# Half of w_out prepared in the first FFN layer, and the second layer's operands kept in trace order: an attention, MoE and FFN chain on one Trainium2 core

## The chip, the cores and the metric

One NeuronCore of one Trainium2 chip runs one launch of the kernel. The metric is the device time of that core in microseconds (us); lower is better. The engines are TensorE (PE; its weight loads are PEld), VectorE (DVE), ScalarE (ACT), GpSimd (POOL) and SyncE (SP), which here only issues DMAs. ScalarE issues DMAs too.

## The reference

Three stages follow one another, all in float32.

```python
def _attn_ref(q, k, v, omega):              # 4 batches, 8 heads, 576 tokens, 64 wide, 128 features
    q_p, k_p = phi(q * scale), phi(k * scale)   # phi: exp(proj - |x|^2/2 - max) / sqrt(m)
    kv = np.einsum('bhsm,bhsd->bhmd', k_p, v)
    num = np.einsum('bhsm,bhmd->bhsd', q_p, kv)
    den = np.einsum('bhsm,bhm->bhs', q_p, z)[..., None] + 1e-06
    return num / den

def _moe_ref(x, w_gate, w1, w2):            # x 2304 x 512, 8 experts, 512 -> 1024 -> 512, top 1
    for e in range(E):
        xe = x[expert_idx == e]
        out[mask] = gate_w[mask, None] * (np.maximum(xe @ w1[e], 0.0) @ w2[e])

def _moe2_ref(x, w_in, w_out):              # 2304 x 512, w_in 512 x 2048, w_out 2048 x 512
    h = x @ w_in
    g = h * (1.0 / (1.0 + np.exp(-1.702 * h)))
    return g @ w_out
```

The weights w_in and w_out of the last stage lie in HBM as 8-byte floating point numbers.

## The kernel before

**Stages.** The attention and the MoE of earlier batches are interleaved on TensorE until some 346 us from the span's start (a batch's MoE takes the one expert that most of its tokens chose, for all its tokens; tokens of other experts would go through a loop at the end, which does not run with these inputs). The MoE of the last batch ends at 420 us. Then the last stage runs as two layers: the first layer (x by w_in, then the gate function) until 601 us, the second (by w_out) until 794 us.

**The two layers.** Both use a two by two block scheme with 7 products in place of 8, and each product takes three fp32r matmuls (high by high, high by low, low by high part), so that every operand is split into a high part, made by a ScalarE copy (L817), and a low part, made by a VectorE subtraction (L818), by the helper `split`. The first layer has 8 column groups j and 3 token sets t: 24 pairs of 42 matmuls with 384 columns, written by `first(j, t)` (L1097). The second has 9 token blocks k of 168 matmuls with 256 columns, 24 for each product, written by `second(k)` (L1198). For block k the operands are the parts of g (tiles gt and pg, read back from g_dram): a11, a12, a22 as they are, and sums and differences of them (`made`, L1184). The order of products in both layers is 1, 7, 5 (or 6), 6, 2, 4, 3; `ops[n]` are the two halves of product n's operand, in the tiles gs and p.

**Preparing the weights.** An 8-byte number is turned into a float32 by three integer operations on VectorE (L789, L794 and L798, in `decoding`). `prep_ins` does this for w_in, column group by column group, mixes the blocks (L864, `tt`) and splits them into wi. `prep_outs` does it for w_out: for each of 8 groups j, two loads (raw_o), 2 times 3 decoding operations of 128x512, four mixes (L864, z from z) of 128x256, and two stores from z to wo_dram (L926, L927). z and raw_o live in the pool wz, whose two tiles later hold the wi of group 0. `prep_w(i)` (L1153) later loads one product's w_out operand from wo_dram (p or pw) and splits it; it waits, when the kernel is written out, until all 8 groups are done (`outs[0] < NP`).

**What sets the order.** A list of generators (`Runner`, `jobs`) is advanced one tick at a time from the loops that write out the matmuls; in the first layer there are 7 ticks per pair. Each `yield n` in a generator lets n ticks go by. Behind this a scheduler reorders the instructions of each engine by its own estimate, except those that `behind(ins, n)` keeps behind the last n instructions that were written before them on their engine (HOLD is 1). In `second` the operands are held in this way for blocks 0 to 2 only (`HOLD if k < 3 else 0`), and the VectorE half of `split` never is. All loads of w_out and the stores to wo_dram are on SP's queue; the stores of g (g_dram) are on ScalarE's queue. `g` tiles of the first layer (tag "ob") rotate through three buffers, and a buffer is free again when the store of the g that it held has landed. y_t[t] are the operands of token set t; the loop over `order` waits (in writing) for wi of j and y of t.

**Matmuls.** In the first layer a pair of the products' writes goes `pa`, `pq`, `pf` and so on (PSUM tiles qa, qm, qn or qt, qu); VectorE adds two of them into g or qn or qt (L864), ScalarE applies the gate function (L1105).

In `second(k)` the four leading steps (`ops[1]`; s1; a21; `ops[7]`) of block k+1 are written in step 6 of block k, its last product:

```python
                if step == 6 and k + 1 < NB2:
                    for _ in range(4):
                        next(blocks[k + 1])
```

## Time and profile before

| | |
|---|---|
| Time, median of 3 runs (us) | 798.47 (793.82 to 801.49) |
| The profiled execution (us) | 802.5 |
| Its span in the trace (us) | 800.7 |
| TensorE busy | 755.4 us, 94% of the span |
| VectorE busy | 530.4 us, 66% |
| ScalarE busy | 340.4 us, 43% |
| GpSimd busy | 132.5 us, 17% |

The profiled execution is one more run than the three, and its time has 1.8 us outside the span. Times in rows are microseconds from the span's start. A busy engine is one with an instruction in progress; the idle time in square brackets behind a row is that just before it on its engine, with what ended it. PEclk is the clock that TensorE was granted, as a share of 2.4 GHz; it has two levels, 0.5 and 1. L numbers are lines of the kernel before; in the changed kernel the same lines are one further from about line 818 on, and more later.

### The profile page before, as it was taken

Reading aid. Unit: us, or ns where it says so; the run is one execution under the profiler, and the core shown is the slowest. Engines: PE = TensorE matmul, PEld = TensorE weight load, DVE = VectorE, ACT = ScalarE, POOL = GpSimd, SP = SyncE. Lnnn points to the kernel's source line nnn. Section 1 sums busy time; section 2 is a strip of 40 time slices with the busy share of each in tenths; the row PEclk is TensorE's granted clock in tenths of the full one; section 3 lists DMA queues with packets and bytes.
Section 4 is the critical chain, followed back from the end, with each engine's and each line's share of the span. In section 5 each row is a group of like instructions: output and inputs, shape, how many; then the busy total and the mean of one; then the engine's idle time right before and its main releaser. Section 6 shows DMA issues by size and latency. Waiting matters only on the chain.

```text
span 800.7 us, 14405 instructions
## 1 busy us (share of the span) xinstructions
PE 755.4 (94%) x5589; PEld 728.7 (91%) x5589; DVE 530.4 (66%) x1178; ACT 340.4 (43%) x643; POOL 132.5 (17%) x78
## 2 busy tenths in 40 slices
PE   7998899996999898999999999999999989999996
PEld 6877799996999888999999999998999889999996
DVE  5867786576988775435869825544358677777761
ACT  5545562343423422243417644544566233433330
POOL 4554295356300422000000000000000000000000
PEclk9989899999899999999999999999999989999999
DMA  6446674268864864167236435443779343444211
GB/s 157 128 111 170 197 216 121 74 165 241 243 183 157 215 237 137 50 185 240 74 123 202 161 119 173 149 178 119 289 276 318 116 132 120 144 130 135 80 27 31
DMA packets 135724, 126.59 MB, mean 158 GB/s; under 512 B 57568, under 2 KB 120288, under 8 KB 134752
## 3 DMA queue, kind: packets, MB, share of 16 engines
q1 hardware_dynamic: 128736, 106.72, 44.6%
q10 hardware_dynamic: 6912, 18.88, 6.2%
q8 instruction: 46, 0.75, 0.4%
q14 instruction: 30, 0.25, 0.1%
HBM read 78.69 MB, written 40.39 MB: 149 GB/s over the span
## 4 chain that ended last, share of the span: by engine, by line
PE 45%; DVE 5%; DMA 3%; issue 1%; ACT 1%; DVEq 0%; ACTq 0%; SPq 0%
PE qa L1198 12%; PE qa L1097 11%; PE qm L1198 7%; PE m_ps L126 3%; PE pb L1198 3%; PE qm L1097 3%; PE qu L1097 2%; PE w_ps L126 2%; DMA g_dram<-g 2%; PE qn L1097 1%; PE qt L1097 1%; DVE y L818 1%; DVE p L818 1%; DMA gt<-g_dram 1%; DVE gs L818 1%
## 5 line engine op out<-in xcount | busy, mean ns | idle before, releaser
L1097 PE MATMUL qa<-y,wi 128*128 128x384 f32 x576 | 109.0, 336 | 3.5 <-DVE g L864 2.1
L1097 PEld LDWEIGHTS qa<-y,wi 128*128 128x128 f32 x576 | 100.2, 188 | 5.7 <-DVE g L864 3.4
L126 PE MATMUL m_ps<-xh,wh 128*128 128x288 f32 x256 | 80.4, 314 | 1.8 <-DVE h1l L698 1.7
L126 PE MATMUL m_ps<-xh,wl 128*128 128x288 f32 x256 | 78.1, 305 | 0.0
L126 PE MATMUL m_ps<-xl,wh 128*128 128x288 f32 x256 | 77.7, 304 | 0.0
L663 POOL TENSOR_TENSOR wl<-st,wh 128x1024 fp32r<-128x1024 f32 x23 | 55.5, 2421 | 111.3 <-ACT wh L661 111.2
L347 DVE TENSOR_REDUCE small<-pr 128x4 f32<-128x512 f32 (+1 forms) x80 | 51.1, 639 | 10.3 <-PE pr L339 3.9
L126 PEld LDWEIGHTS m_ps<-xh,wh 128*128 128x128 f32 x256 | 50.3, 196 | 3.0 <-DVE h1l L698 2.9
L661 ACT ACTIVATE wh<-st 128x1024 fp32r<-128x1024 f32 (+1 forms) x33 | 34.0, 1033 | 39.6 <-DMA st<-in_moe_w_dram 33.0
L126 PEld LDWEIGHTS m_ps<-xl,wh 128*128 128x128 f32 x256 | 50.2, 196 | 0.1
L126 PEld LDWEIGHTS m_ps<-xh,wl 128*128 128x128 f32 x256 | 49.9, 195 | 0.2
L695 ACT ACTIVATE h1h<-m_ps 128x288 fp32r<-128x288 f32 x64 | 25.8, 406 | 56.3 <-PE m_ps L126 56.2
L698 DVE SCALAR_TENSOR_TENSOR h1l<-m_ps,h1h 128x288 fp32r<-128x288 f32 x64 | 28.7, 452 | 30.1 <-ACT h1h L695 29.9
L126 PE MATMUL m_ps<-h1h,wh 128*128 128x288 f32 x160 | 48.4, 303 | 0.0
L126 PE MATMUL m_ps<-h1l,wh 128*128 128x288 f32 x160 | 47.9, 300 | 0.0
L126 PE MATMUL m_ps<-h1h,wl 128*128 128x288 f32 x160 | 47.7, 299 | 0.0
L1198 PE MATMUL qa<-p,p 128*128 128x256 f32 x360 | 45.8, 284 | 1.1 <-DVE p L818 0.9
L1198 PEld LDWEIGHTS qa<-p,p 128*128 128x128 f32 x360 | 44.3, 192 | 1.6 <-DVE p L818 1.1
L1198 PE MATMUL qa<-p,gs 128*128 128x256 f32 x360 | 45.3, 283 | 0.0
L1198 PEld LDWEIGHTS qa<-p,gs 128*128 128x128 f32 x360 | 44.1, 192 | 0.0
L432 PEld LDWEIGHTS num<-kv,qpT 128*128 128x128 f32 (+1 forms) x320 | 37.5, 187 | 6.3 <-ACT qpT L420 2.7
L432 PE MATMUL num<-kv,qpT 128*128 128x65 f32 (+1 forms) x320 | 40.1, 269 | 3.0 <-ACT qpT L420 1.0
(208 smaller groups left out, 1845.8 us busy)
## 6 DMA issues: line engine op xcount, KB each, us to landing
g_dram<-g ACTq DMA_DIRECT2D x48, 384.0 KB, 2.6
st<-in_moe_w_dram SPq DMA_DIRECT2D x31, 512.0 KB, 5.4
pg<-g_dram SPq DMA_DIRECT2D x10, 1024.0 KB, 5.7
raw_o<-in_moe_w_out_dram SPq DMA_DIRECT2D x16, 512.0 KB, 3.9
raw<-in_moe_w_in_dram SPq DMA_DIRECT2D x16, 512.0 KB, 4.4
gt<-g_dram SPq DMA_DIRECT2D x8, 1024.0 KB, 5.5
wo_dram<-z SPq DMA_DIRECT2D x8, 768.0 KB, 6.5
p<-wo_dram SPq DMA_DIRECT2D x6, 1024.0 KB, 7.5
```

The costliest lines, as they stand in the source:

```text
L126: ins = nc.tensor.matmul(out=ps, lhsT=a, rhs=b, start=start and n == 0, stop=stop and n == 2)
L347: nc.vector.tensor_reduce(out=pm, in_=ps[:, :w], axis=AX.X, op=ALU.max, negate=on_act)
L432: nc.tensor.matmul(out=ps[:n, c, h2, :], lhsT=lhsT, rhs=kv[:, h, :])
L661: nc.scalar.activation(out=hi[:, :, s], in_=st[:, :, s], func=ACTF.Copy)
L663: eng.tensor_tensor(out=lo[:, :, s], in0=st[:, :, s], in1=f32(hi)[:, :, s], op=ALU.subtract)
L695: nc.scalar.activation(out=hh[:, f], in_=ps, func=ACTF.Relu)
L698: nc.vector.scalar_tensor_tensor(out=hl[:, f], in0=ps, scalar=0.0, in1=f32(hh[:, f]), op0=ALU.max, op1=ALU.subtract)
L818: nc.vector.tensor_tensor(out=lo, in0=src, in1=f32(hi), op=ALU.subtract)
L1097: ins = nc.tensor.matmul(out=ps, lhsT=w[:, a, ks], rhs=y[:, b, kk], start=start and kk + m == 0, stop=kk == 1 and m == 2, skip_group_check ...
L1198: ins = nc.tensor.matmul(out=ps, lhsT=x[:, f], rhs=w[i][:, f], start=start and f + m == 0, stop=f == NP - 1 and m == 2, skip_group_check=True,
```

## The change

It has five parts.

1. `prep_outs` takes its groups, its tiles and its queue as arguments. Groups 0 to 3 are prepared in the attention, from tick 245 of its clock on instead of from the first finished batch on, with loads and stores on ScalarE's queue. Groups 4 to 7 are prepared in the first layer, on SP's queue, in the tile that held yt, from the moment y_t[2] is made. Each group has three stores instead of two.
2. `prep_ins` starts its loads and its decoding without waiting for w_out; it waits for groups 0 to 3 before it writes to wi. Its pace goes from 8 to 6 ticks, and it yields after every second mix.
3. The first nine pairs are done set by set, (0,0), (1,0), (2,0), (0,1) and so on, instead of (0,0), (1,0), (0,1), (1,1), (2,0).
4. In `second` both halves of an operand, and the sums, are held in trace order for all blocks. The four leading steps of a block are written two in step 5 and two in step 6 of the block ahead.
5. The paces of `prep_w` for the third and fourth operand go from 10 and 13 to 7 and 9.

```diff
+    NP1 = 4
+    OUT_FROM = 245
-    IN_PACE = 8
+    IN_PACE = 6
...
-    def split(hi, lo, src, n=0):
+    def split(hi, lo, src, n=0, n_lo=0):
         behind(nc.scalar.activation(out=hi, in_=src, func=ACTF.Copy), n)
-        nc.vector.tensor_tensor(out=lo, in0=src, in1=f32(hi), op=ALU.subtract)
+        behind(nc.vector.tensor_tensor(out=lo, in0=src, in1=f32(hi), op=ALU.subtract), n_lo)
...
-        while outs[0] < NP:
-            yield 1
         raw = [load(0, 0), load(1, 0)]
...
-            while j % 3 >= len(slots["wi"]) or (j > 2 and through[j - 3] < NSET):
+            while j % 3 >= len(slots["wi"]) or (j > 2 and through[j - 3] < NSET) or outs[0] < NP1:
                 yield 1
...
+    def prep_outs(js, qs, ts, raws, queue, gap):
...
+            behind(queue.dma_start(out=raws[n], in_=w_out[f * P:(f + 1) * P, :]), 1)
...
+            for o, n, x in ((0, 1, q[:, 0:1]), (1, 2, q[:, 2:4]), (3, 4, ts)):
+                behind(queue.dma_start(out=wo_dram[o:o + n, :, j].rearrange("o p d -> p o d"), in_=x), 1)
             outs[0] += 1
-            yield OUT_PACE
+            yield gap
...
-            if x_done[0]:
+            if clock[0] >= OUT_FROM:
                 jobs()
...
             def made(out, x, y, op):
-                behind(nc.vector.tensor_tensor(out=out, in0=x, in1=y, op=op), HOLD if k < 3 else 0)
+                behind(nc.vector.tensor_tensor(out=out, in0=x, in1=y, op=op), HOLD)
...
-                split(gs[:, 0], gs[:, 1], x, n)
+                split(gs[:, 0], gs[:, 1], x, HOLD, HOLD)
...
-        order = [(0, 0), (1, 0), (0, 1), (1, 1), (2, 0), (2, 1), (0, 2), (1, 2), (2, 2)]
+        order = [(j, t) for t in range(NSET) for j in range(3)]
...
         def after_group(j, t):
+            if "late" not in slots and 2 in y_t:
+                slots["late"] = p = ly.tile([P, ZW], F32, tag="yt", name="pz", bufs=1)
...
+                jobs.queue.append(prep_outs(
+                    range(NP1, NP), (z[:, 0:4], z[:, 4:8]), z[:, 8:12], (raws[:, 0], raws[:, 1]), nc.sync, 3
+                ))
...
-                jobs.queue += [prep_w(2, p[:, 0:WO], 10), prep_w(3, p[:, WO:2 * WO], 13)]
+                jobs.queue += [prep_w(2, p[:, 0:WO], 7), prep_w(3, p[:, WO:2 * WO], 9)]
...
-                if step == 6 and k + 1 < NB2:
-                    for _ in range(4):
+                if step > 4 and k + 1 < NB2:
+                    for _ in range(2):
                         next(blocks[k + 1])
+                if step == 6:
                     if k + 2 < NB2:
                         gts[k + 2] = load_g(k + 2)
```

Three places show what moves.

On VectorE in the attention, the rows of the kernel before where the first group of w_out begins (mx, qp, small: steps of the attention's features; z: w_out):

```order
L347 TENSOR_REDUCE small<-pr 128x4
L789 TENSOR_SCALAR z<-raw_o 128x512
L356 TENSOR_TENSOR small<-small,sq 128x4
L794 SCALAR_TENSOR_TENSOR z<-raw_o,z 128x512
L356 TENSOR_TENSOR mx<-small,sq 128x4
L798 SCALAR_TENSOR_TENSOR z<-raw_o,z 128x512
L368 TENSOR_TENSOR qp<-pr,mx 128x512
```

and the same place in the changed kernel:

```order
L348 TENSOR_REDUCE small<-pr 128x4
L357 TENSOR_TENSOR small<-small,sq 128x4
L357 TENSOR_TENSOR mx<-small,sq 128x4
L369 TENSOR_TENSOR qp<-pr,mx 128x512
L348 TENSOR_REDUCE small<-pr 128x2
```

The three z rows between the feature steps are gone from here; the changed kernel's first z row stands about 150 VectorE rows further on, between rows of the MoE (h1l).

On ScalarE in the MoE of the last batch, the rows of the changed kernel that read the staged expert weights (wh) and its hidden part (h1h); the kernel before has the wh and h1h rows alone:

```order
L908 DMA raw_o_233<-in_moe2_w_out_dram 128x512 x2
L662 ACTIVATE wh0_4380<-st_4158 128x1024
L696 ACTIVATE h1h_4343<-m_ps_4404 128x288
L696 ACTIVATE h1h_4343<-m_ps_4423 128x288
L662 ACTIVATE wh1_4419<-st_4179 128x1024
L696 ACTIVATE h1h_4343<-m_ps_4440 128x288
L926 DMA wo_dram_77<-z_232 128x256
L662 ACTIVATE wh2_4455<-st_4402 128x1024
L696 ACTIVATE h1h_4343<-m_ps_4459 128x288
L926 DMA wo_dram_77<-z_232 128x2x256
L662 ACTIVATE wh3_4491<-st_4438 128x1024
```

Loads of w_out and stores to wo_dram now stand in ScalarE's own order, each store ahead of a split that TensorE needs.

On VectorE in the second layer, the rows of the kernel before around the seventh operand of block 2 (p0 from pg is its low half; s1_7276 is a sum of block 2, s1_7481 and the gt1 rows are the leading steps of block 3):

```order
L1184 TENSOR_TENSOR s1_7276<-pg_6524 128x1024
L1211 TENSOR_TENSOR ob_7216<-qm_7136,pg_6524 128x256
L1184 TENSOR_TENSOR s1_7481<-gt1_6892 128x1024
L1184 TENSOR_TENSOR pg_6524<-pg_6524 128x8x128
L1211 TENSOR_TENSOR ob_7215<-qa_7163,pg_6524 128x256
L818 TENSOR_TENSOR p1_6714<-s1_7276,p1_6714 128x1024
L1184 TENSOR_TENSOR gt1_6892<-gt1_6892 128x8x128
L818 TENSOR_TENSOR gs_6851<-pg_6524,gs_6851 128x1024
L818 TENSOR_TENSOR p0_6523<-pg_6524,p0_6523 128x1024
```

and in the changed kernel (the names' numbers are 9 higher):

```order
L1185 TENSOR_TENSOR s1_7259<-pg_6533 128x1024
L1212 TENSOR_TENSOR ob_7225<-qm_7145,pg_6533 128x256
L1185 TENSOR_TENSOR pg_6533<-pg_6533 128x8x128
L1212 TENSOR_TENSOR ob_7224<-qa_7172,pg_6533 128x256
L819 TENSOR_TENSOR p0_6532<-pg_6533,p0_6532 128x1024
L819 TENSOR_TENSOR p1_6723<-s1_7259,p1_6723 128x1024
L1185 TENSOR_TENSOR s1_7259<-s1_7259,pg_6533 128x1024
```

Between the difference a21 (pg from pg) and the low half of the seventh operand (p0 from pg) stood four other rows, one of them block 3's (gt1) and one the low half of a later operand (p1); now one stands there.

## Rows read from the trace of the kernel before

**Rows 1.** The head of the page and its engines (busy us, share, instructions).

```profile
span 800.7 us, 14405 instructions
...
PE 755.4 (94%) x5589; PEld 728.7 (91%) x5589; DVE 530.4 (66%) x1178; ACT 340.4 (43%) x643; POOL 132.5 (17%) x78
```

**Rows 2.** Stretch, length, busy (instructions) of PE, PEld, DVE, ACT, POOL; PEclk, DMA share, GB/s.

```profile
187.00:262.00 75.00, 68.83 (x589) 65.79 (x589) 67.27 (x201) 25.78 (x54) 17.98 (x8) 0.95 0.67 203
262.00:346.00 84.00, 77.27 (x582) 73.87 (x581) 52.57 (x153) 25.33 (x52) 19.76 (x8) 0.96 0.52 157
420.20:601.10 180.90, 177.35 (x1014) 175.02 (x1013) 98.98 (x162) 99.24 (x187) 0.00 (x0) 1.00 0.52 184
601.10:794.40 193.30, 186.85 (x1513) 185.43 (x1511) 135.93 (x146) 74.75 (x86) 0.00 (x0) 0.97 0.40 127
```

**Rows 3.** What TensorE waited for (total us, times, longest).

```profile
PE tq L418 <- DVE qp L368: 9.9, 6, 4.6
...
PE qm L1198 <- DVE p L818: 3.3, 1, 3.3
...
PE qm L1198 <- DVE gs L818: 1.8, 1, 1.8
```

**Rows 4.** Timeline of TensorE, 193.5 to 200.5 us.

```profile
199.13 1.09 PE L418 MATMUL tq<-ident,qp 128*128 128x128 f32 x4 [4.62 <-DVE qp L368]
```

**Rows 5.** Timeline of VectorE, 192 to 200 us.

```profile
191.72 2.12 DVE L789 TENSOR_SCALAR z<-raw_o 128x512 int32<-128x512 int32 x1 [0.31 <-DMA raw_o<-in_moe_w_out_dram]
...
193.87 2.72 DVE L794 SCALAR_TENSOR_TENSOR z<-raw_o,z 128x512 int32<-128x512 int32 x1
...
198.30 0.68 DVE L368 TENSOR_TENSOR qp<-pr,mx 128x512 f32<-128x512 f32 x1
```

**Rows 6.** The tile z: one operation's durations (min, median, max ns).

```profile
L794 DVE SCALAR_TENSOR_TENSOR z<-raw_o,z x16: 672/683/2718, 193.9 to 322.9; 128x512 int32<-128x512 int32 x16
```

**Rows 7.** Timeline of GpSimd, 192 to 200 us.

```profile
193.50 2.54 POOL L663 TENSOR_TENSOR wl<-st,wh 128x1024 fp32r<-128x1024 f32 x1
```

**Rows 8.** Stretches behind waits, columns as in rows 2.

```profile
199.13:205.10 5.97, 5.97 (x33) 5.81 (x33) 5.90 (x17) 2.30 (x4) 2.38 (x1) 0.50 0.71 210
...
628.40:631.90 3.50, 3.46 (x16) 3.46 (x17) 2.38 (x3) 1.06 (x1) 0.00 (x0) 0.52 0.02 4
...
653.86:659.00 5.14, 5.14 (x24) 5.14 (x25) 3.43 (x3) 1.06 (x1) 0.00 (x0) 0.50 0.51 164
659.00:679.00 20.00, 20.00 (x168) 20.00 (x168) 13.13 (x15) 7.85 (x9) 0.00 (x0) 1.00 0.41 129
270.00:273.40 3.40, 3.40 (x17) 3.40 (x16) 3.40 (x7) 1.47 (x2) 2.26 (x1) 0.50 0.55 142
```

**Rows 9.** Timeline of TensorE at three waits of the two layers.

```profile
430.28 2.02 PE L1097 MATMUL qa<-y,wi 128*128 128x384 f32 x10 [0.92 <-DVE g L864]
...
544.07 0.61 PE L1097 MATMUL qa<-y,wi 128*128 128x384 f32 x2 [1.10 <-ACT wi L817]
...
653.86 1.44 PE L1198 MATMUL qm<-p 128*128 128x256 f32 x5 [3.27 <-DVE p L818]
```

**Rows 10.** Timeline of VectorE, 645.5 to 654.5 us.

```profile
651.45 1.22 DVE L818 TENSOR_TENSOR gs<-pg,gs 128x1024 fp32r<-128x1024 f32 x1
652.59 1.22 DVE L818 TENSOR_TENSOR p<-pg,p 128x1024 fp32r<-128x1024 f32 x1
```

**Rows 11.** Timeline of VectorE at the first layer's end, 583 to 602 us.

```profile
599.32 0.55 DVE L864 TENSOR_TENSOR g<-qa,qs 128x384 f32<-128x384 f32 x1
```

**Rows 12.** Timeline of VectorE, 264 to 276 us.

```profile
266.62 0.43 DVE L789 TENSOR_SCALAR z<-raw_o 128x512 int32<-128x512 int32 x1 [3.78 <-DMA wo_dram<-z]
```

**Rows 13.** Timeline of VectorE, 480 to 505 us.

```profile
487.41 0.56 DVE L864 TENSOR_TENSOR g<-qa,qs 128x384 f32<-128x384 f32 x1 [3.05 <-DMA g_dram<-g]
```

**Rows 14.** Timeline of GpSimd, 262 to 313 us.

```profile
262.05 4.71 POOL L663 TENSOR_TENSOR wl<-st,wh 128x1024 fp32r<-128x1024 f32 x2 [48.11 <-ACT wh L661]
```

**Rows 15.** Timeline of ScalarE, 340 to 372 us.

```profile
354.91 1.06 ACT L661 ACTIVATE wh<-st 128x1024 fp32r<-128x1024 f32 x1 [4.25 <-DMA st<-in_moe_w_dram]
```

More of the change, by code (lines that the diff above doesn't have):

```diff
@@ L885, in prep_ins @@
             s1, s2, s4 = (mix[:, i] for i in range(3))
-            for o, x, y, op in (
+            for n, (o, x, y, op) in enumerate((
                 (s1, dec[:, WS3], dec[:, W22], ALU.add), (dec[:, WS3], dec[:, W11], dec[:, WS3], ALU.subtract),
                 (s2, s1, dec[:, W11], ALU.subtract), (s4, dec[:, W12], s2, ALU.subtract),
-            ):
+            )):
                 behind(tt(nc.vector, o, x, y, op), HOLD)
-                yield 1
-            while j % 3 >= len(slots["wi"]) or (j > 2 and through[j - 3] < NSET):
+                if n % 2:
+                    yield 1
+            while j % 3 >= len(slots["wi"]) or (j > 2 and through[j - 3] < NSET) or outs[0] < NP1:
                 yield 1
@@ L902 @@
     outs = [0]
-    def prep_outs():
-        z = wz.tile([P, 8 * HD], F32, tag="a", name="z", bufs=1).rearrange("p (o d) -> p o d", o=8)
-        zi = z.bitcast(I32)
-        raws = wz.tile([P, 2, DM], I64, tag="b", name="raw_o", bufs=1)
+    def prep_outs(js, qs, ts, raws, queue, gap):
         def load(n, j):
             f = j + n * NP
-            behind(nc.sync.dma_start(out=raws[:, n], in_=w_out[f * P:(f + 1) * P, :]), 2)
-        load(0, 0)
-        load(1, 0)
+            behind(queue.dma_start(out=raws[n], in_=w_out[f * P:(f + 1) * P, :]), 1)
+        load(0, js[0])
+        load(1, js[0])
         yield 8
-        for j in range(NP):
+        for i, j in enumerate(js):
+            q = qs[i % len(qs)]
+            qi = q.bitcast(I32)
             for n in range(2):
-                yield from decoding(zi[:, 2 * n:2 * n + 2].rearrange("p a c -> p (a c)"), raws[:, n])
-            for i, (o, a, b, op) in enumerate(O_MIX):
-                if j + 1 < NP and not i % 2:
-                    load(i // 2, j + 1)
-                behind(tt(nc.vector, z[:, o], z[:, a], z[:, b], op), HOLD)
+                yield from decoding(qi[:, 2 * n:2 * n + 2].rearrange("p a c -> p (a c)"), raws[n])
+            z = [q[:, o] for o in range(4)] + [ts[:, o] for o in range(4)]
+            for m, (o, a, b, op) in enumerate(O_MIX):
+                if m % 2 and i + 1 < len(js):
+                    load(m // 2, js[i + 1])
+                behind(tt(nc.vector, z[o], z[a], z[b], op), HOLD)
                 yield 1
             yield 1
-            behind(nc.sync.dma_start(out=wo_dram[0, :, j], in_=z[:, 0]), 2)
-            behind(nc.sync.dma_start(out=wo_dram[1:7, :, j].rearrange("o p d -> p o d"), in_=z[:, 2:8]), 1)
+            for o, n, x in ((0, 1, q[:, 0:1]), (1, 2, q[:, 2:4]), (3, 4, ts)):
+                behind(queue.dma_start(out=wo_dram[o:o + n, :, j].rearrange("o p d -> p o d"), in_=x), 1)
             outs[0] += 1
-            yield OUT_PACE
+            yield gap
     def prep_y(t, home, after=0):
@@ L976 @@
         jobs = Runner(4)
-        jobs.queue.append(prep_outs())
+        z = wz.tile([P, 8 * HD], F32, tag="a", name="z", bufs=1).rearrange("p (o d) -> p o d", o=8)
+        raws = wz.tile([P, 2, DM], I64, tag="b", name="raw_o", bufs=1)
+        jobs.queue.append(prep_outs(range(NP1), (z[:, 0:4],), z[:, 4:8], (raws[:, 0], raws[:, 1]), nc.scalar, 7))
         a_live = True
@@ L1183, in made, with halves_of @@
             def made(out, x, y, op):
-                behind(nc.vector.tensor_tensor(out=out, in0=x, in1=y, op=op), HOLD if k < 3 else 0)
+                behind(nc.vector.tensor_tensor(out=out, in0=x, in1=y, op=op), HOLD)
                 return out
-            def halves_of(x, n=0):
+            def halves_of(x):
                 gs = gs_homes[operands[0] % 5].rearrange("p (s f n) -> p s f n", s=2, f=NP)
                 operands[0] += 1
-                split(gs[:, 0], gs[:, 1], x, n)
+                split(gs[:, 0], gs[:, 1], x, HOLD, HOLD)
                 return gs[:, 0], gs[:, 1]
@@ L1218, in second @@
             last = k == NT // (2 * P) - 1
-            ops = {1: halves_of(a11, HOLD if k < 3 else 0)}
+            ops = {1: halves_of(a11)}
             yield
@@ L1285, with leading @@
         blocks = []
+        def leading(n):
+            for _ in range(n):
+                next(blocks[0])
+                yield 2
         def after_group(j, t):
+            if "late" not in slots and 2 in y_t:
+                slots["late"] = p = ly.tile([P, ZW], F32, tag="yt", name="pz", bufs=1)
+                z = p[:, 0:12 * HD].rearrange("p (o d) -> p o d", d=HD)
+                raws = p[:, 12 * HD:12 * HD + 4 * DM].bitcast(I64).rearrange("p (n c) -> p n c", n=2)
+                jobs.queue.append(prep_outs(
+                    range(NP1, NP), (z[:, 0:4], z[:, 4:8]), z[:, 8:12], (raws[:, 0], raws[:, 1]), nc.sync, 3
+                ))
             if (j, t) == (7, 0):
@@ L1305, in after_group @@
                 gs_homes.extend(wz.tile([P, GSW], F32R, tag=tag, name="gs", bufs=1) for tag in ("a", "b"))
-            for _ in range({(7, 1): 2, (5, 2): 2, (6, 2): 2}.get((j, t), 0)):
+            if (j, t) in ((7, 1), (5, 2)):
+                jobs.queue.append(leading(2))
+            if (j, t) == (6, 2):
+                next(blocks[0])
                 next(blocks[0])
```

1 line of the change is left out of this document (removed).

## The prediction

> **What bounds the kernel now.** I read the head of the page first: TensorE is busy for 755.4 of 800.7 us and VectorE for 530.4 [rows 1]. So the time is TensorE's work plus its gaps plus what it does at half clock, and an edit here is worth what it takes from the last two. No part of the change adds or removes a matmul. Next the busy time by stage [rows 2]: TensorE idles 75.00 - 68.83 = 6.2 us in 187 to 262, 6.7 us in 262 to 346 and 193.30 - 186.85 = 6.5 us in the second layer. In the first of these VectorE is busy for 67.27 of 75.00, so there it is nearly a bound itself; in 262 to 346 it has 31 us free. The waits of TensorE then name the releasers: VectorE's qp for 9.9 us in 6 waits, one of 4.6, and in the second layer two single waits of 3.3 and 1.8 us for low halves (p and gs, L818) [rows 3]. Last, the timeline around each of these.
>
> The longest is at 199.13 us [rows 4]: TensorE waits for qp at 198.30, and ahead of qp on VectorE stand three w_out operations of group 0, of which 2.12 and 2.72 us are shown [rows 5]. An L794 takes 683 ns in the median and 2718 at most [rows 6]; the long ones run while GpSimd is in an operation of 2.54 us [rows 7]. Behind that wait the granted clock is 0.50, the 1.2 GHz level, for 5.97 us [rows 8]; at the full level that work would take about half, so some 3.0 us go with it. The same pair, a wait and then half clock, stands in the second layer: TensorE waits until 653.86 [rows 9] and then does 24 matmuls in 5.14 us, where 168 take 20.00 us at full clock, 0.119 each [rows 8]. That loses 5.14 - 24 x 0.119 = 2.3 us.
>
> **The change part by part.** The profiled execution took 802.5 us, 4.0 above the median of the three runs (798.47). The sum is made against 802.5 and then laid on the median.
>
> *Second layer's operands in trace order.* In block 2 the low half of the seventh operand starts at 652.59, behind the low half of gs, which is wanted later [rows 10], and behind steps of block 3. In the new order one row of 0.42 us and no split stands between the difference and it, so it is done some 3 x 1.14 us earlier, and the wait of 3.3 and the half clock of 2.3 behind it go: -5.7 with what is left between instructions. In block 1 the same low half follows its difference directly: the wait of 1.8 us [rows 3] and about 0.3 before it fall to about 1.0 (the difference and the low half, 1.14 each, less what the product ahead covers). Behind it 16 matmuls took 3.50 us [rows 8], so 3.5 - 16 x 0.119 = 1.6 go too: -2.9 with rounding. What is late next are the third operand of block 0 (a wait that stays) and, from block 3 on, the seventh operand: its chain is one sum, one difference and two splits in two products' time of 2.88 us each, with VectorE 70% busy there (135.93 of 193.30 [rows 2]), so I see no new wait. Sum: -8.6. From both sides: -9.5 if block 0's wait goes too, +3 if a held row waits for a late g and holds the next operand.
>
> *First layer, its end and its start.* The second and third operand of w_out are brought forward by the shorter paces and stand, in VectorE's new order, between the last two g. In the rows of before the last g starts at 599.32 [rows 11]; five more operations of about 1.14 us fall ahead of it, of which some 3.4 us of free time take most, so it comes about 1.7 us later: +1.7. The g before last now stands ahead of a sum instead of behind it: -0.6. At the start, wi of group 2 is wanted one pair earlier than it was, and a decoding step moves ahead of the g that TensorE already waits for, 0.92 us, at 430.28 [rows 9]: +1.5. The waits for wi of group 7, 1.10 us at 544.07 [rows 9] and, as I estimate it, 0.7 behind it for the low half of the same wi, go because the pace of w_in's preparation is 6 instead of 8: -1.8. Together +0.8.
>
> *Groups 4 to 7 in the first layer.* A group is 4 operations of 0.68 [rows 6] and 6 short ones of about 0.43 [rows 12], 5.3 us, four groups 21 us of VectorE, which is busy for 98.98 of 180.90 us in the first layer [rows 2]; the free 82 us hide them, and if they did not, one ahead of a g would cost up to 0.7 us each time. Their transfers do meet the stores of g: once, before, a g waited 3.05 us until such a store had landed and given its buffer free [rows 13], and TensorE's list of waits has no entry behind it. Bounds: 0, and about nine pairs, over which the four groups spread, with one such wait each, of which TensorE feels 1 us as far as I can judge (the wait less the product of two us that covers it). I take +1, near the one row that there is.
>
> *Groups 0 to 3 late in the attention.* In 187 to 262 nothing of w_out is left: the wait of 4.6 [rows 3] and the 3.0 of half clock behind it go: -7.6. The other 1.6 us of that stretch's idle time is a wait for the tokens' low half and stays. In 262 to 346 there were groups 3 (its end) to 7 and there will be groups 0, 1 and part of 2. Before, its 6.7 us of idle time hold a wait of 3.78 for the store of z [rows 12] and two long w_out operations, with two stretches of half clock of 3.4 us (one shown [rows 8]), 1.7 lost in each: 10.1 in all. In the busy part of it, until about 305, three groups stood and two will: GpSimd still splits expert weights there, 4.71 us for two [rows 14]. I keep two thirds as lost and one third as won, -3.3. From both sides: -10.1, if fewer operations meet GpSimd, and 0, if each meets as many.
>
> The Trainium skill, "SBUF — State Buffer", section "SBUF: two separate sides", says that VectorE and GpSimd share a port pair that is locked for a whole instruction, the loser waiting. The durations here [rows 5, 6] beside GpSimd's [rows 7] agree. By that rule what counts is how often an operation starts beside GpSimd's, and the six weight splits of 262 to 305 are still there: the one third would be nothing, and the sum 3.3 us higher.
>
> *ScalarE's queue.* 8 loads and 12 stores move from SP's queue to ScalarE's. SP loses them and nothing waits for it. ScalarE is 25.33 us busy in 84.00 [rows 2], so the issuing alone is covered. But a store waits on ScalarE for VectorE's z, and the splits of expert weights (wh) and of the hidden part (h1h) are queued behind it, for which TensorE waits. In the last batch's MoE there is room: one wh waits 4.25 us for its load anyway [rows 15]. Bounds: 0, and 2.0 us (the excess of a long z operation, 2.72 - 0.68 [rows 5, 6]) for each of 12 stores, 24. I take +2, one such excess that reaches TensorE, since most z operations are at their median.
>
> Sum: -8.6 + 0.8 + 1 - 7.6 - 3.3 + 2 = -15.7. On the profiled execution 786.8, on the median 782.8; I say 783.
>
> **The rivals.**
>
> *Only the layers gain.* The w_out work in the attention meets GpSimd and the softmax steps elsewhere and stalls as often. For it: GpSimd's six splits in 262 to 305, and an order of the attention that changes as a whole. Against: half the groups have left the attention. Then -8.6 + 0.8 + 1 = -6.8: 791.7.
>
> *All of the attention's loss goes.* All of 7.6 and 10.1, ScalarE's queue free: -8.6 + 1.8 - 17.7 = -24.5: 774.
>
> *Transfers hold g.* Nine us in the first layer, one a pair, in place of the 1 counted: -15.7 + 8 = -7.7: 790.8. For it: that wait of 3.05 [rows 13]. Against: TensorE did not wait behind it.
>
> *Slower: ScalarE stands behind the stores.* Place: the batch b = 2 and 3 experts, 262 to 362 us. A store waits for z, wh or h1h behind it comes late, TensorE idles and falls to half clock. Price: as the one seen, 4.6 + 3.0 = 7.6 for each of four groups = 30.4, against 17.7 that go: +12.7, with the layers' -6.8 making +5.9: 804.4; if a group stops it twice, up to 830. It decides from the point where more than three such stops (24.5 / 7.6) fall on the path. Against it: most stores stand several rows behind their z.
>
> **How the numbers follow.** Forecast 0.46, only the layers 0.19, all goes 0.13, transfers 0.10, slower 0.12. A measurement of this kernel tells about 1%, 8 us, from no change. Faster by over 1% (under 790.5): the forecast, all goes, and about half of the cases near 791, 0.72. Within 1%: the rest of those, the forecast's upper edge and a third of the slower rival, 0.20. Slower: 0.08. The range goes from 772, below "all goes", to 796, above both cases near 791, and leaves out the slower rival and some of the far end.
>
> **What would show it.** Right: no half clock near 199, the wait for qp under 2 us there; in the second layer waits of at most about 1 us behind L818 in blocks 1 and 2 and no PEclk under 0.9; a first wait near the last g. Wrong: idle of ScalarE ahead of wh or h1h released by VectorE's z; waits of g for g_dram in 460 to 540; TensorE's idle time in 262 to 346 at 6.7 us or more; any wait in blocks 3 to 8.

## The result and the profile after

| | before | changed |
|---|---|---|
| Time, median of 4 runs each (us) | 796.14 (793.79 to 801.49) | 773.35 (772.88 to 775.22) |
| The profiled execution (us) | 802.5 | 772.88 |
| Its span (us) | 800.7 | 770.9 |
| First matmul of the first layer (us) | 420.8 | 399.5 |
| First matmul of the second layer (us) | 601.1 | 580.8 |
| Last matmul's end (us) | 794.4 | 765.6 |

The ratio is 0.9709, with a 95% interval of 0.965 to 0.9767: faster by 2.9%, 22.8 us by the medians. The forecast was 783; the time came out at the rival "all of the attention's loss goes" (774), 1.4 us above the low end of the range (772). The two profiled executions lie further apart (29.6 us) than the medians, since that of before, 802.5, was slower than its four timed runs.

Line numbers of the changed kernel are one higher than before in all rows shown, not only behind line 818 (L347 is L348, L1198 is L1199). The head of its page answers to [rows 1]:

```profile
span 770.9 us, 14408 instructions
...
PE 742.6 (96%) x5589; PEld 716.3 (93%) x5589; DVE 532.5 (69%) x1178; ACT 338.7 (44%) x643; POOL 131.8 (17%) x78
```

TensorE has the same 5589 matmuls in 12.8 fewer busy us (matmuls at half clock, granted 0.50 or 1.2 GHz, count as busy for longer) and idles 28.3 us in place of 45.3. VectorE is as busy as before.

The stages answer to [rows 2] (stretch, length, busy us and instructions of PE, PEld, DVE, ACT, POOL, granted clock, DMA share, GB/s). The same work begins some 3 us earlier here at the first of them, and ends 20 us earlier at the last but one:

```profile
184.00:262.00 78.00, 76.45 (x679) 72.92 (x679) 53.70 (x176) 28.80 (x61) 22.42 (x11) 1.00 0.46 125
262.00:304.00 42.00, 41.36 (x325) 39.63 (x325) 33.66 (x72) 13.74 (x27) 13.49 (x6) 1.00 0.51 161
304.00:346.00 42.00, 40.24 (x296) 38.26 (x296) 23.25 (x77) 13.37 (x26) 0.00 (x0) 1.00 0.52 158
...
399.50:580.80 181.30, 177.32 (x1010) 174.44 (x1009) 117.09 (x201) 98.94 (x188) 0.00 (x0) 1.00 0.65 228
580.80:765.60 184.80, 182.64 (x1514) 181.62 (x1512) 134.59 (x144) 72.58 (x85) 0.00 (x0) 1.00 0.43 133
```

Read them by TensorE's idle time and the clock. In 184 to 262 it idles 1.6 us (before, in 187 to 262, 6.2 at a clock of 0.95), in 262 to 304 only 0.6 (before 6.7), and the clock is 1.00 in each of these stages. In 304 to 346 it idles 1.8 us where it had no idle time before; so some of the waits have moved and not gone. The first layer took 181.3 us (before 180.3), the second 184.8 (before 193.3). So the profiled pair differs by 21.2 us ahead of the first layer, by -1.0 in it, by 8.5 in the second and by 1.0 behind. Of the 21.2, 3.4 were there before the changed work begins (TensorE's 1350th matmul starts at 180.4 us in place of 183.8): the execution of before has two stretches of half clock in 40 to 95 us, the one after a single one. The other 17.8 us are the attention's and the MoE's gain in this pair of executions; the runs below put it at about 14 between medians.

TensorE's waits answer to [rows 3]:

```profile
PE m_ps L127 <- DVE h1l L699: 2.7, 5, 0.7
PE qa L1098 <- DVE g L865: 2.7, 5, 1.0
PE tq L419 <- DVE qp L369: 2.1, 3, 1.1
...
PE qm L1199 <- DVE gs L819: 0.8, 1, 0.8
```

The wait for qp is 2.1 us in three pieces where it was 9.9 with one of 4.6; the wait of 3.3 in block 2 is gone, and the one of 1.8 in block 1 is 0.8.

One thing stayed that should have cost. The w_out operations (tile z: count, then shortest, median and longest in ns) are still stretched:

```profile
L795 DVE SCALAR_TENSOR_TENSOR z<-raw_o,z x8: 676/689/2280, 257.8 to 338.2; 128x512 int32<-128x512 int32 x8
L799 DVE SCALAR_TENSOR_TENSOR z<-raw_o,z x8: 681/688/2766, 258.5 to 338.9; 128x512 int32<-128x512 int32 x8
```

The longest, 2.77 us, is as long as the longest before [rows 6]. Yet TensorE idles for 0.6 us in all of 262 to 304. The longest of them stands ahead of an h1l on VectorE, and TensorE waits 0.34 us for that h1l (two rows of VectorE, one of TensorE):

```profile
288.54 2.77 DVE L799 SCALAR_TENSOR_TENSOR z<-raw_o,z 128x512 int32<-128x512 int32 x1
291.23 0.45 DVE L699 SCALAR_TENSOR_TENSOR h1l<-m_ps,h1h 128x288 fp32r<-128x288 f32 x1
...
291.73 0.40 PE L127 MATMUL m_ps<-xh,wh 128*128 128x288 f32 x1 [0.34 <-DVE h1l L699]
```

So a long operation is not yet a large loss, and the experiments have to tell what made it one.

### The profile page after: what moved, and what is told of

Read it like the earlier page. It is cut to its first block, busy times and chain, and to the rows that moved or that the text cites. A ratio compares the mean times of both kernels' runs of the same rounds, so it can differ in the third digit from the quotient of the medians.

```text
span 770.9 us, 14408 instructions
## 1 busy us (share of the span) xinstructions
PE 742.6 (96%) x5589; PEld 716.3 (93%) x5589; DVE 532.5 (69%) x1178; ACT 338.7 (44%) x643; POOL 131.8 (17%) x78
## 4 chain that ended last, share of the span: by engine, by line
PE 72%; DVE 11%; DMA 9%; ACT 3%; issue 2%; SPq 1%; POOL 1%; ACTq 0%; DVEq 0%; POOLq 0%
PE m_ps L127 16%; PE qa L1199 13%; PE qa L1098 10%; PE qm L1199 7%; DMA st<-in_moe_w_dram 4%; PE pb L1199 3%; PE w_ps L127 3%; PE num L433 3%; PE qu L1098 2%; DMA g_dram<-g 2%; PE qm L1098 2%; PE kv_ps L391 2%; PE pr L333 2%; DMA m<-in_k_dram 2%; PE tq L419 1%
## 5 line engine op out<-in xcount | busy, mean ns | idle before, releaser
L127 PE MATMUL m_ps<-xh,wh 128*128 128x288 f32 x256 | 78.5, 307 | 2.1 <-DVE h1l L699 2.0
L127 PE MATMUL m_ps<-xh,wl 128*128 128x288 f32 x256 | 76.1, 297 | 0.0
L127 PE MATMUL m_ps<-xl,wh 128*128 128x288 f32 x256 | 75.5, 295 | 0.0
L348 DVE TENSOR_REDUCE small<-pr 128x4 f32<-128x512 f32 (+1 forms) x80 | 51.1, 639 | 13.0 <-PE pr L340 5.0
L127 PEld LDWEIGHTS m_ps<-xh,wh 128*128 128x128 f32 x256 | 48.1, 188 | 3.6 <-DVE h1l L699 3.2
L127 PEld LDWEIGHTS m_ps<-xl,wh 128*128 128x128 f32 x256 | 48.1, 188 | 0.0
L127 PEld LDWEIGHTS m_ps<-xh,wl 128*128 128x128 f32 x256 | 48.1, 188 | 0.0
L1199 PE MATMUL qa<-p,p 128*128 128x256 f32 x360 | 46.5, 284 | 1.1 <-DVE p L819 0.9
L1199 PE MATMUL qa<-p,gs 128*128 128x256 f32 x360 | 46.3, 283 | 0.0
L1199 PEld LDWEIGHTS qa<-p,p 128*128 128x128 f32 x360 | 44.5, 192 | 1.6 <-DVE p L819 1.1
L1199 PEld LDWEIGHTS qa<-p,gs 128*128 128x128 f32 x360 | 44.6, 192 | 0.0
```

What stands on the lines that cost most here:

```text
L127: ins = nc.tensor.matmul(out=ps, lhsT=a, rhs=b, start=start and n == 0, stop=stop and n == 2)
L348: nc.vector.tensor_reduce(out=pm, in_=ps[:, :w], axis=AX.X, op=ALU.max, negate=on_act)
L1199: ins = nc.tensor.matmul(out=ps, lhsT=x[:, f], rhs=w[i][:, f], start=start and f + m == 0, stop=f == NP - 1 and m == 2, skip_group_check=True,
```

## The experiments

Each ran in three rounds against the kernel before; times are medians, the range of the runs in brackets. The changed kernel was run again as a yardstick among them. The kernel before had medians of 796.8 to 798.7 in these sets, so a difference between runs of different sets is given by medians and, where it matters, also by the ratios to the kernel before, times 798 us. Where the two disagree, by up to 1.6 us, the size is known no better than that.

**The changed kernel once more.**

> The changed kernel itself, as the yardstick for the others of this set: 772 to 776, ratio to the kernel before 0.965 to 0.977.

774.82 us (773.81 to 775.9), ratio 0.9705 (0.9665 to 0.9744). Over both sets its eight runs lie between 772.88 and 775.9.

### Where the attention's gain comes from

**All 8 groups early again.**

```diff
-    NP1 = 4
+    NP1 = 8
-            if clock[0] >= OUT_FROM:
+            if x_done[0]:
-        jobs.queue.append(prep_outs(range(NP1), ..., nc.scalar, 7))
+        jobs.queue.append(prep_outs(range(NP1), ..., nc.sync, 5))
-            if "late" not in slots and 2 in y_t:
+            if "late" not in slots and 2 in y_t and NP1 < NP:
```

> All 8 groups of w_out in the attention again, from the first finished batch on, on SyncE's queue at the old pace; all the rest of the change stays. Theory A (the change's gain ahead of the first layer, 21 us in the profiled executions, comes from the w_out operations on VectorE among the attention's steps): the waits for qp near 199 and 302 us and their half clock return, the first layer starts 14 to 18 us later than in the changed kernel, the first layer wins about 1 us; time 787 to 791. Theory B (much of the 21 us is a difference between executions, as the 3.4 us by which the changed kernel is ahead at 184 us already): the first layer starts 7 to 11 us later; time 780 to 784.

788.97 us (783.16 to 793.82), ratio 0.9884 (0.982 to 0.9949): 14.2 us above the changed kernel (14.3 by the ratios). Its first layer starts at 416.6 us, 17 later than in the changed kernel. Theory A holds, with the late wait at 299 us for an xn and not for a qp. Its waits of TensorE (total, times, longest):

```profile
PE tq L419 <- DVE qp L369: 7.5, 4, 5.2
...
PE m_ps L127 <- DVE h1l L699: 3.2, 2, 2.5
PE num L433 <- DVE xn L444: 2.9, 1, 2.9
```

and its stages, columns as above:

```profile
184.00:262.00 78.00, 72.17 (x623) 69.12 (x623) 69.63 (x209) 27.26 (x58) 19.70 (x10) 0.96 0.65 200
262.00:310.00 48.00, 42.59 (x312) 41.48 (x311) 35.31 (x80) 13.29 (x25) 17.01 (x7) 0.89 0.71 233
```

TensorE idles 5.8 us in the first stretch and 5.4 in the second, where the clock is 0.89. The wait of 2.5 for h1l stands behind this row of VectorE:

```profile
265.41 1.68 DVE L790 TENSOR_SCALAR z<-raw_o 128x512 int32<-128x512 int32 x1 [3.50 <-DMA wo_dram<-z]
267.00 0.81 DVE L699 SCALAR_TENSOR_TENSOR h1l<-m_ps,h1h 128x288 fp32r<-128x288 f32 x2
```

Here a decoding operation waits 3.50 us until the store of the group before it has left z, is then stretched to 1.68, and the MoE's h1l stands behind it in VectorE's order. That is the row of [rows 12] again. The wait of 2.9 for xn at 299 us has no store in it; two long operations stand ahead of that xn:

```profile
294.08 1.74 DVE L795 SCALAR_TENSOR_TENSOR z<-raw_o,z 128x512 int32<-128x512 int32 x1
...
295.88 2.70 DVE L799 SCALAR_TENSOR_TENSOR z<-raw_o,z 128x512 int32<-128x512 int32 x1
...
298.84 0.41 DVE L444 TENSOR_TENSOR xn<-num,rd 128x256 f32<-128x256 f32 x1
```

**Half of them early, on the same queue.** As the run above, with `NP1 = 4` and the late half in the first layer; VectorE's order is the same up to the end of group 3.

> Groups 0 to 3 as in the kernel before in place and queue (first finished batch, SyncE, old pace), groups 4 to 7 in the first layer: VectorE's order is that of the run with all 8 groups early up to about 265 us, and has no w_out operation from there to the first layer. Theory (each wait belongs to the w_out operations in front of it): the wait near 197 us of about 5 us and its half clock stay (7 to 8 us), the waits near 267 and 299 us of 2.5 and 2.9 us and the half clock behind them go; first layer at about 407 us, time 780 to 783. Rival (the waits of 262 to 305 are the attention's own): they stay, time 786 or more.

778.98 us (777.33 to 781.66), ratio 0.9778 (0.9724 to 0.9833). The theory holds in the trace: the wait at 195 us stays, and those near 267 and 299 us go. The time is 1 us under the range that was expected for it, and the first layer starts at 403.35 us where 407 was expected.

```profile
PE tq L419 <- DVE qp L369: 7.6, 4, 5.3
```

```profile
184.00:262.00 78.00, 72.74 (x629) 69.61 (x629) 68.31 (x207) 27.84 (x59) 19.71 (x10) 0.96 0.65 192
262.00:300.00 38.00, 38.00 (x312) 36.98 (x311) 18.98 (x56) 13.61 (x24) 16.03 (x7) 1.00 0.37 115
```

As many matmuls and transposes (312) as took 48 us with all groups early are done in 38.00 us, without any idle time. So the two runs part the attention's 14.2 us: 10.0 us (788.97 to 778.98) for the second half of the groups, and 4.2 us (778.98 to 774.82) for the place and the queue of the first half. By the ratios the two are 8.5 and 5.8. No run of the one kernel lies within the runs of the next, so that each part is worth something is clear; how much each is worth is less so. (With the 10.1 us of the second layer's run below, 24.3 us are accounted for; the yardstick run is 23.9 us faster than the kernel before in its set.) The three operations in front of the wait are these:

```profile
187.51 2.09 DVE L790 TENSOR_SCALAR z<-raw_o 128x512 int32<-128x512 int32 x1 [0.99 <-DMA raw_o<-in_moe_w_out_dram]
...
189.64 2.71 DVE L795 SCALAR_TENSOR_TENSOR z<-raw_o,z 128x512 int32<-128x512 int32 x1
...
192.38 1.76 DVE L799 SCALAR_TENSOR_TENSOR z<-raw_o,z 128x512 int32<-128x512 int32 x1
194.07 0.68 DVE L369 TENSOR_TENSOR qp<-pr,mx 128x512 f32<-128x512 f32 x1
```

**Half of them early, on ScalarE's queue.** Only the line with `x_done` is put back.

> Groups 0 to 3 on ScalarE's queue as in the change, but from the first finished batch on (about 187 us) instead of from tick 245; groups 4 to 7 stay in the first layer. Theory A1 (what counts is where the operations start: at 190 us VectorE is nearly full and GpSimd busy): the wait of about 4.6 us and 3 us of half clock come back, time 779 to 783, with 262 to 305 free of waits. Theory A2 (what counts is that there are half as many): 772 to 776.

777.41 us (774.58 to 779.67), ratio 0.9757 (0.9727 to 0.9786). The median is between the two theories, 2.6 us above the changed kernel, but the runs of the two overlap, so a difference is likely and not shown. In the profiled execution, the fastest of the four, TensorE waits 2.31 and 2.18 us for kp and qp at 188 and 194 us, there is no half clock behind them, and the first layer starts 2.1 us later than in the changed kernel.

**Half of them where GpSimd rests.**

```diff
-    OUT_FROM = 245
+    OUT_FROM = 205
-        jobs.queue.append(prep_outs(range(NP1), ..., nc.scalar, 7))
+        jobs.queue.append(prep_outs(range(NP1), ..., nc.scalar, 0))
```

> Groups 0 to 3 without gaps from tick 205, which is about 213 us, where GpSimd has nothing to do until about 249 us, while the attention's steps are still dense on VectorE. Theory A3 (it is the meeting with GpSimd that stretches a w_out operation and then holds the attention): the operations up to 249 us take their 0.42 and 0.68 us, no wait over 1 us, time 772 to 776. Theory A4 (it is VectorE's own load in the attention): waits for qp or kp of 2 us and more return in 213 to 262, time 777 to 781.

775.81 us (774.53 to 780.09), ratio 0.9725 (0.9674 to 0.9776): not to be told from the changed kernel. The trace says more than the time. GpSimd's last operation before the pause and its first behind it:

```profile
205.22 2.37 POOL L664 TENSOR_TENSOR wl<-st,wh 128x1024 fp32r<-128x1024 f32 x1 [5.35 <-ACT wh L662]
250.82 2.36 POOL L664 TENSOR_TENSOR wl<-st,wh 128x1024 fp32r<-128x1024 f32 x1 [43.23 <-ACT wh L662]
```

In between, from 220.6 to 246 us, 20 operations on z take their shortest times (0.42 and 0.68 us, 0.41 for a mix), the attention's steps stand among them, and TensorE has no wait. The first one behind the pause is long again, and was late for another reason before that:

```profile
251.91 1.55 DVE L790 TENSOR_SCALAR z<-raw_o 128x512 int32<-128x512 int32 x1 [2.17 <-DMA wo_dram<-z]
```

VectorE waits 2.17 us for the store of the group before it (there is one z in the attention, and this run leaves no gap between groups), and TensorE waits 2.71 us for an xn at 254.67, with half clock behind it. So theory A3 holds up to 249 us: VectorE can take the w_out operations between the attention's steps while GpSimd rests. Behind that point both a meeting with GpSimd and a wait for a store stand ahead of the xn, and this run does not tell them apart.

**The queue alone.**

```diff
-        jobs.queue.append(prep_outs(range(NP1), ..., nc.scalar, 7))
+        jobs.queue.append(prep_outs(range(NP1), ..., nc.sync, 7))
```

> Only the queue of groups 0 to 3 goes back to SyncE, their time and number stay. If ScalarE's queue neither helps nor hurts: within 2 us of the changed kernel, 771 to 776. If waiting stores on ScalarE cost what the prediction put on them (2 us): 770 to 772. If they keep SyncE's loads of expert weights free of waits for z: 777 or more, with later loads of st.

777.42 us (774.46 to 778.91), ratio 0.9741 (0.9706 to 0.9776). The interval overlaps that of the changed kernel, so no difference is shown, and the stores on ScalarE do not cost what was put on them: without them nothing gets faster. The median lies in the third case that was expected (777 or more), but its sign, later loads of st, is not seen: the one longer wait of TensorE, 1.73 us for an h1h at 350.5 us, stands behind a wh that waits 2.29 us for its load, and the wh in that place waits 2.53 us in the changed kernel.

### The second layer

One edit that bears on it is not among the five parts: the leading steps of block 0 come one every two ticks of the job list (`leading`), and not two at once. No run undoes it.

**Its part of the change undone.**

```diff
-                behind(nc.vector.tensor_tensor(out=out, in0=x, in1=y, op=op), HOLD)
+                behind(nc.vector.tensor_tensor(out=out, in0=x, in1=y, op=op), HOLD if k < 3 else 0)
-                split(gs[:, 0], gs[:, 1], x, HOLD, HOLD)
+                split(gs[:, 0], gs[:, 1], x, n)
-                if step > 4 and k + 1 < NB2:
-                    for _ in range(2):
+                if step == 6 and k + 1 < NB2:
+                    for _ in range(4):
```

> The whole fourth part undone (holding only in blocks 0 to 2, leading steps all in the last product), the rest stays. Theory: the waits of about 1.8 and 3.3 us for low halves in blocks 1 and 2 return with half clock behind them, second layer 193 us instead of 184.8, time 780 to 783. Rival (the second layer is faster because w_out's operands come earlier by the paces): second layer 185 to 188, time 773 to 777.

784.96 us (783.74 to 787.91), ratio 0.9848 (0.9813 to 0.9883): 10.1 us above the changed kernel (11.4 by the ratios). The second layer, and in it the stretch behind the wait in block 2:

```profile
584.30:778.20 193.90, 187.07 (x1513) 185.64 (x1512) 132.78 (x144) 72.60 (x85) 0.00 (x0) 0.97 0.39 126
637.28:642.80 5.52, 5.52 (x26) 5.52 (x27) 3.42 (x3) 1.06 (x1) 0.00 (x0) 0.50 0.59 181
```

The waits are those of before, 1.81 and 3.28 us, and 26 matmuls take 5.52 us at half clock as in [rows 8].

**Only the holding undone,** the spread stays.

> Of the fourth part only the holding goes back (low halves free for the scheduler, all of it free from block 3 on); the leading steps stay spread over two products. Theory (the order of the low halves is what counts): in block 2 the low half of the seventh operand stands behind two other splits again, waits of 2 to 3.5 us and half clock return there, time 778 to 783, second layer 189 to 193 us. Rival (the spread alone takes the waits away): second layer under 187 us, time 773 to 777.

785.46 us (782.89 to 787.13), ratio 0.9845 (0.9787 to 0.9904). All of the loss is back.

```profile
PE qa L1098 <- DVE g L865: 4.9, 5, 2.6
...
PE qm L1199 <- DVE p L819: 3.3, 1, 3.3
...
PE qm L1199 <- DVE gs L819: 1.8, 1, 1.8
```

The first row shows a second effect. Where the low halves are free, one more of them (gs) and a sum go ahead of the first layer's last g, and TensorE waits 2.6 us there as well; the run before this one has the same wait at 583.13 us.

**Only the spread undone,** the holding stays.

> Of the fourth part only the spread goes back: all four leading steps in the last product, all held in trace order. Theory: the operand's chain of a sum, a difference and two splits (about 1.2 + 1.1 + 1.1 + 1.1 us) has one product of 2.88 us in place of two, so waits of 1 to 2 us come at the head of several blocks, second layer 188 to 196 us, time 778 to 786. Rival (holding alone suffices): second layer under 187 us, 773 to 777.

779.02 us (774.61 to 780.62), ratio 0.9775 (0.9719 to 0.9831). The waits are smaller than the theory had them, 0.76 us in block 2 and, from block 3 on, one stop in each of six blocks, in which a matmul starts 0.42 us behind the one ahead instead of 0.12, with some 0.2 us in smaller pieces around it. The second layer takes 188.74 us in place of 184.80:

```profile
578.56:767.30 188.74, 184.97 (x1513) 182.37 (x1512) 135.20 (x144) 71.76 (x85) 0.00 (x0) 1.00 0.42 130
```

The lengths of the second layer, from its first matmul to the last one's end, are 193.7 us with neither (the window shown for that run ends 0.2 us later), 193.7 with the spread alone, 188.8 with the holding alone and 184.8 with both. So holding alone gives 4.9 us and the spread 4.0 on top of it; without the holding the spread gives nothing. (By the medians the holding alone gives 5.9 and the spread 4.2; the runs of this one overlap the changed kernel's at one end.)

### The first layer

**The first pairs in the old order.**

```diff
-        order = [(j, t) for t in range(NSET) for j in range(3)]
+        order = [(0, 0), (1, 0), (0, 1), (1, 1), (2, 0), (2, 1), (0, 2), (1, 2), (2, 2)]
```

> Only the order of the first nine pairs goes back. The prediction put +1.5 us on the first layer's start in the new order: then this is 1 to 2 us faster in 400 to 430 us (waits of 0.98, 0.57 and 0.38 shrink to one of about 1), time 771 to 774. Rival (the new order is needed, because the sets' operands come later): a wait for y of set 1 of 2 us or more, time 776 or more.

772.86 us (771.27 to 773.95), ratio 0.9672 (0.9632 to 0.9711). In the same set the changed kernel had 774.82; the intervals overlap, so the 2 us are not shown. In the profiled executions the waits at the layer's start are 0.97 and 0.98 us with the old order, and 0.97, 0.57 and 0.49 with the new one (in the yardstick run): no gain of the new order is to be seen.

**w_in's pace back.**

```diff
-    IN_PACE = 6
+    IN_PACE = 8
```

> Only the pace of w_in's preparation goes back from 6 to 8. Theory: the wait for wi of group 7 returns, 1.8 us or a little more since the late w_out operations now share VectorE: 775 to 777, a wait L1098 on wi of 1 to 3 us near 522 us. Rival (it was another edit that took the wait away): no such wait, 772 to 775.

777.69 us (777.05 to 779.09), ratio 0.9742 (0.9702 to 0.9782): 2.9 us above the changed kernel. All its runs are slower than all eight of the changed kernel. Neither theory had it right: the loss is there, but no wait for wi of group 7. Instead the decoding of w_in and that of the late w_out come together at 494 to 500 us, with a wait for a store of g between them:

```profile
493.46 0.56 DVE L865 TENSOR_TENSOR g<-qa,qs 128x384 f32<-128x384 f32 x1 [2.37 <-DMA g_dram<-g]
```

TensorE waits 0.75 us for that g and 1.37 for the qn that follows, which stands behind five decoding operations and three low halves of wi on VectorE.

**The old order of pairs and the old paces of w_out's third and fourth operand.**

```diff
-        order = [(j, t) for t in range(NSET) for j in range(3)]
+        order = [(0, 0), (1, 0), (0, 1), (1, 1), (2, 0), (2, 1), (0, 2), (1, 2), (2, 2)]
-                jobs.queue += [prep_w(2, p[:, 0:WO], 7), prep_w(3, p[:, WO:2 * WO], 9)]
+                jobs.queue += [prep_w(2, p[:, 0:WO], 10), prep_w(3, p[:, WO:2 * WO], 13)]
```

> The first pairs in the old order and the paces of the third and fourth w_out operand back at 10 and 13, all else as changed. The prediction put +1.7 - 0.6 on the first layer's end by these paces: then the waits for qt and g near 577 and 580 us go, the second layer's start may wait for an operand instead; time 770 to 773. Rival (w_out's operands then come too late for the second layer): second layer over 187 us, time 775 or more.

770.59 us (769.6 to 772.43), ratio 0.9671 (0.9617 to 0.9725). It is the fastest of all: its four runs lie below all eight of the changed kernel (772.88 and more), though the ratios' intervals overlap. The waits for qt and g at the layer's end, 0.52 and 0.35 us in the changed kernel, are gone, and the second layer is longer by 0.2 us (the second window below ends 0.2 us behind the last matmul):

```profile
397.65:577.50 179.85, 176.22 (x1010) 174.62 (x1009) 114.33 (x198) 96.55 (x184) 0.00 (x0) 1.00 0.65 229
577.50:762.70 185.20, 182.62 (x1513) 181.60 (x1512) 137.86 (x148) 74.83 (x89) 0.00 (x0) 1.00 0.42 132
```

The first layer takes 179.85 us against 181.30 and 182.43 in the two traces of the changed kernel. Of the five parts of the change, the third and the fifth are thus not seen to bring anything; which of the two costs something this run, with both undone, cannot tell.

## Why the prediction was right, and where its sum was off

**The range held the time, near its edge.** The forecast was 9.7 us too slow. The time came where the prediction had put a rival with a chance of 0.13, and the range holds it because it was drawn down to just below that rival. The second layer's mechanism came as it was written; the attention gained as forecast in kind, but its sum was wrong in the split and in the size of its terms.

**Second layer, forecast -8.6.** Right: the terms as written (3.3 + 2.3, and 1.8 + 0.3 - 1.0 + 1.6) sum to 8.3, so 0.3 of the 8.6 are rounding, and the stage gave 8.5 us between the profiled executions, with the remaining waits where they were foretold (0.8 in block 1, none in block 2, the one of block 0 unchanged). Undone, it costs 10.1 us, one to two of them at the first layer's end.

**First layer, forecast +0.8, and +1 for the late groups.** Together +1.0 in the profiled pair, in place of +1.8. The late groups are hidden, as said. The end's term was a little too dear: it was to lose 1.7 - 0.6, and the waits of that stretch sum up to 1.57 us (0.70, 0.52 and 0.35) where they were 1.01 (0.71 and 0.30). The step that was only half right is the pace of w_in (-1.8). Of the 1.8, the 0.7 estimated for the low half of wi is 0.36 in the trace of before; and undoing the pace costs 2.9 us, but not through the wait for wi of group 7.

The rival "transfers hold g" did not come. In the profiled execution of the changed kernel the longest such wait, 4.17 us, leaves TensorE 0.26 us of idle time:

```profile
549.57 0.56 DVE L865 TENSOR_TENSOR g<-qa,qs 128x384 f32<-128x384 f32 x1 [4.17 <-DMA g_dram<-g]
```

A wait of this kind near the layer's end costs more: in the second trace of the changed kernel a g waits 3.68 us for a store of g,

```profile
572.96 0.56 DVE L865 TENSOR_TENSOR g<-qa,qs 128x384 f32<-128x384 f32 x1 [3.68 <-DMA g_dram<-g]
```

and the wait for the qt behind it is 1.62 us in place of 0.52. It costs about 1 us there, not 1 in each of nine pairs, and the loads that were issued shortly before it (at 559 and 568 us) are those of w_out's operands p and pw, not those of the late groups.

**The attention, forecast -7.6 - 3.3 + 2 = -8.9, measured -14.2.** This is where the sum failed, in its split and in all three of its terms. (Between the two profiled executions the gain is 17.8 us, as much as the 17.7 that the rival took; the execution of before was slower than all four timed runs.)

The failing step is "I keep two thirds as lost and one third as won, -3.3" for 262 to 305. The groups that left that stretch were worth 10.0 us by medians and 8.5 by the ratios, near the other end of the bounds given for it (-10.1). The prediction took the loss as shared among the groups standing there, as if every long w_out operation cost the same. The traces show otherwise: seven long operations, 1.41 to 2.77 us each, stand in 255 to 292 in the changed kernel, and TensorE waits 0.34 us behind the longest and for none of the others. In the kernel before there are nine over 0.7 us, and two waits for qp of 4.6 and 2.8 us stand behind them.

The seven waits of more than 2.5 us in 190 to 310 us, over all traces, have one thing in common: several delays stand ahead of one step that TensorE needs. In the three at 195 to 199 us these are three long operations. At 299 and 302 us (all groups early, and the kernel before) they are two. At 267 us (all groups early) and 255 us (from tick 205) they are a wait for a store and one long operation. A stretch of half clock goes with each of the seven. So a wait for a store is one such delay, but not a needed one. In the changed kernel most long operations stand alone, but two (1.69 and 1.89 us, at 278 and 281 us) stand close together and TensorE has no wait there. How late a step can be before TensorE feels it was not tried and stays open.

The term of -7.6 for the place of group 0 was too large, in the other direction: 4.2 us by medians, 5.8 by the ratios, in the run that puts the place and the queue of groups 0 to 3 back. The wait comes back in its full size (5.26 us) with half clock behind it, but the first layer starts only 3.3 us later than in the yardstick run (403.35 against 400.04). Of the 5.26 us, 3.7 show as additional idle time in 184 to 262 (5.3 against 1.6 in the changed kernel, which has smaller waits of its own there), and behind it this run idles less: not at all in 262 to 300, where the changed kernel has 0.6 in 262 to 304. So the wait and its half clock were an upper bound of what its removal gave.

The +2 for ScalarE's queue did not come. In all fourteen traces here no operation on z took over 0.70 us with GpSimd at rest, and the long ones, up to 2.79 us, all ran beside a GpSimd operation; in the run from tick 205 the 20 operations between 220.6 and 246 us took their shortest times, and the first one beside GpSimd again took 1.55 instead of 0.42. The Trainium skill, "SBUF — State Buffer", section "SBUF: two separate sides", says that a GpSimd operation and a VectorE operation with two SBUF inputs or in a two-port mode lock a shared port pair for the whole instruction, and the traces agree with it for these operations. What was drawn from it, that the third of the attention's gain would vanish because the meetings go on, was wrong: the meetings went on (seven long operations in place of nine), and the loss went.

**The rivals.** "Only the layers gain" needed an attention that stalls as before; 14.2 us say no. "Slower: ScalarE stands behind the stores" has no wait to show: in the profiled execution of the changed kernel TensorE waits for wh nowhere, and for h1h 0.41 us at most.

## What to carry to other kernels

Work of an engine that can be done at any time should stand where two things are absent: another engine beside which its operations are stretched, and a consumer that is on the critical path. In this kernel the time when GpSimd rests was as good a place as a later stage. A single buffer that is emptied by a DMA makes the engine wait in order, with all that is queued behind it (3.50 us here); a gap between the groups that is longer than the store avoids that, and two buffers should, which was not tried in the attention. And a scheduler's freedom is worth taking away where operands are used in a known order: holding them in trace order was worth 5 us of the second layer here, and spreading their steps over two products 4 more, but only once they were held.

## What the hardware showed that was not expected

- VectorE operations on z of 0.42 and 0.68 us took up to 2.79 us while GpSimd was in operations of about 2.4 us, and never more than 0.70 while GpSimd rested; yet seven stretched operations in 255 to 292 us of the changed kernel left TensorE only 0.34 us of waiting.
- Half clock (granted 0.50, 1.2 GHz, for 3.4 to 6.8 us) went with every wait of TensorE of 2.5 us and more in 190 to 310 us and in the second layer. The length of one wait does not tell, though. At the first layer's end one wait of 2.62 us had none (its part of the change undone) and one of 2.64 us had it (only the holding undone). Behind waits of 2.3 and 2.2 us near 190 us (half the groups early, ScalarE's queue) there was none. The wait of 1.81 us in block 1 was followed by it in two of three traces. In the second trace of the changed kernel it came behind two waits of 0.6 and 0.7 us at 331 to 333 us.
- The changed kernel's eight runs spread over 3.0 us, the four of before over 7.7; that it is the waits and their half clock that differ between executions is likely, and not shown.
